# Dummy products in the waits of a gated-mix kernel's start, and a different split of five weight loads over two queues

## The chip, the core and the metric

The kernel runs on one core of a Trainium2 chip. The metric is the device time in microseconds (us) of one execution. Before the change it is 261.29 us, the median of five runs that lie between 261.19 and 261.47 us. One more execution was taken with the hardware profiler, and every row of the profile is from that one.

## The reference

One token block `x` of 2048 rows and 640 columns goes through two branches, which a gate mixes row by row. All arrays are bf16.

```python
g = sigmoid((x * gate_w).sum(-1, keepdims=True))
# branch a: linear attention, 32 heads of 20 columns
q, k, v = split(x @ wqkv)
phi = lambda t: where(t > 0, t + 1, exp(t)) + 1e-6
kv  = einsum("bhsd,bhse->bhde", phi(k), v);  z = phi(k).sum(s)
a   = (phi(q) @ kv / (phi(q) @ z + 1e-6)) @ wo
# branch b: shifted mixer, then an MLP
h  = gelu(layernorm(x) @ w1)
x1 = x + shift_four_column_groups(h) @ w2
b  = x1 + gelu(layernorm(x1) @ w3) @ w4
out = g * a + (1 - g) * b
```

## The kernel before

The 2048 rows are 16 chunks of 128. The order of the work on each engine is the order in which the program is written (`manual_schedule`); engines and queues run beside each other and wait for each other by semaphores.

**The stages.** First comes the projection to `k` for all 16 chunks (`k_mm`, L246, and `k_post`, L251), then `q` in ten units with the products of `phi(k)` and `x` between them, then `w1`, the small products of the attention, `w2`, and at last `w3` and `w4` with the mix. The change touches the loads and the products ahead of the first stage and the first chunk of it.

**The operands of the first stage.** A `k` chunk needs two things. One is the transposed chunk of `x`, in `xT` (the tile RXT): 640 rows on five groups of 128 partitions. The other is the weight for `k`, in `wkg` (the tile RA): five slabs of 128 rows, called wk slab 0 to 4 here, each with 640 columns of weight, one column that holds the gate weight, and one column of ones. So one chunk is 5 x 2 matrix products, one of 512 columns and one of 130 for each slab, added up in one of four PSUM buffers `PP[0]` to `PP[3]`. For chunk c of the loop, ScalarE takes exp and copies the last two columns out, and VectorE finishes `phi` with two instructions.

**How the operands come.** Two queues issue loads, SyncE's (SP) and ScalarE's. ScalarE's queue issues the gate row (`g5`, L160) and then wk slabs 1 and 3. SP's queue issues chunk 0 of `x` as it stands in memory (`load_x`, L155), then wk slabs 0, 2 and 4 (`load_wk`, L164), and then, in `late_loads`, the transposing loads of `x` (`load_xT`, L158): chunks 1 to 5 one by one and chunks 6 to 15 in pairs, which write `xT` directly. Behind these stand the loads of `wq`, the other rows of `x` and the weights of the later stages, all on SP's queue.

**Chunk 0.** It doesn't wait for a transposing load: TensorE transposes it from `x_sb` in five products (L318), VectorE copies three of the results to `xT` (L319) and ScalarE two (L320). The gate row is transposed in the same way (L310) and VectorE puts it into `wkg` (L311). Between these, TensorE multiplies constant ones by ones into a part of PSUM that nothing reads (`warm_up`, L304): three such products of 512 columns at the start, one of 512 and one of 128 behind the gate's transpose, and the same two behind the transposes of `x`. Then the loop over chunks starts at L326.

```python
    load_x(0, 1)
    for (q, dc) in ((aq, 1), (sp, 0), (aq, 3), (sp, 2), (sp, 4)):
        load_wk(q, dc)
```

Of the kernel before, what the change touches and what calls it, by code (L numbers as in the profile page):

```python
# [16 lines left out]
def kernel(  # L17
# [14 lines left out]
    P = 128  # L32
# [3 lines left out]
    NCH = S // P  # L36
    DC = D // P
# [97 lines left out]
    PP = [psum.tile([P, 1024], F32, name=f"pp{i}") for i in range(4)]  # L135
    free = [0, 1, 2, 3]

    def alloc():
        return free.pop(0)

    def release(i):
        free.append(i)

    mm = nc.tensor.matmul
# [6 lines left out]
    sp, aq = nc.sync, nc.scalar  # L151
    xv = x2.rearrange("(c p) d -> p c d", p=P)

    def load_x(c0, c1):
        sp.dma_start(x_sb[:, c0:c1, :], xv[:, c0:c1, :])  # L155
# [7 lines left out]
    def load_wk(q, dc):  # L163
        q.dma_start(wkg[:, dc, 0:D], A_wqkv[dc * P:(dc + 1) * P, D:2 * D])  # L164

    load_x(0, 1)
    for (q, dc) in ((aq, 1), (sp, 0), (aq, 3), (sp, 2), (sp, 4)):
        load_wk(q, dc)


# [66 lines left out]
    def phi(dst, src, n, extra=None):  # L237
        e = eb[ecnt[0] % NE]
        ecnt[0] += 1
        act(e[:, 0:n], src, ACT.Exp)  # L240
        if extra is not None:
            act(extra[0], extra[1], ACT.Copy)
        nc.vector.tensor_scalar(e[:, 0:n], e[:, 0:n], 1.0, 1e-6, op0=ALU.min, op1=ALU.add)  # L243
        nc.vector.scalar_tensor_tensor(dst, src, 0.0, e[:, 0:n], op0=ALU.max, op1=ALU.add)  # L244

    def k_mm(c, p, dc):  # L246
        for (n0, n1) in ((0, 512), (512, KW)):
            mm(PP[p][:, n0:n1], lhsT=xT[:, dc, c * P:(c + 1) * P], rhs=wkg[:, dc, n0:n1],  # L248
               start=(dc == 0), stop=(dc == DC - 1))

    def k_post(c, p):  # L251
        phi(pk[:, c, :], PP[p][:, 0:D], D, (ym[:, c, :], PP[p][:, D:D + 2]))
        release(p)
# [47 lines left out]
    def one(shape):  # L301
        return nc.const_aps.tensor(1.0, shape, BF16)

    def warm_up(n, cols=512):  # L304
        for _ in range(n):
            mm(PP[1][:, 512:512 + cols], lhsT=one([P, P]), rhs=one([P, cols]), start=True, stop=True)

    warm_up(3)
    tg = PP[0][:, 512:1024].bitcast(BF16)
    nc.tensor.transpose(tg[:, 0:DC], g5[0:DC, :], ident[0:DC, 0:DC])  # L310
    nc.vector.tensor_copy(wkg[:, :, D:D + 1], tg[:, 0:DC].rearrange("p (j o) -> p j o", o=1))  # L311
    warm_up(1)
    warm_up(1, 128)

    ta, tb = PP[3][:, 0:512].bitcast(BF16), PP[2][:, 0:512].bitcast(BF16)
    for dc in range(DC):
# [1 line left out]
        nc.tensor.transpose(t[:, k * P:(k + 1) * P], x_sb[:, 0, dc * P:(dc + 1) * P], ident[:])  # L318
    nc.vector.tensor_copy(xT[:, 0:3, 0:P], ta[:, 0:3 * P].rearrange("p (j s) -> p j s", j=3))  # L319
    act(xT[:, 3:5, 0:P], tb[:, 0:2 * P].rearrange("p (j s) -> p j s", j=2), ACT.Copy)  # L320
    warm_up(1)
    warm_up(1, 128)
    free[:] = [1, 0, 3, 2]


    for c in range(NCH):  # L326
        p = alloc()
        for dc in range(DC):
            k_mm(c, p, dc)
        k_post(c, p)  # L330
# [20 lines left out]
    for half in range(2):  # L351
        for j in range(DC):
            p = alloc()
            for dc in range(DC):
                for tt in range(2):
                    t0 = half * 1024 + tt * 512
                    mm(PP[p][:, tt * 512:(tt + 1) * 512], lhsT=wqp[:, dc, j], rhs=xT[:, dc, t0:t0 + 512],  # L357
                       start=(dc == 0), stop=(dc == DC - 1))
# [327 lines left out]
```

## Time and profile before

| what | value |
|---|---|
| median of five runs | 261.29 us (261.19 to 261.47) |
| the profiled execution, device time | 261.53 us |
| the profiled execution, span of the profile | 259.8 us |
| TensorE products, busy | 255.8 us, 98% of the span |
| VectorE busy | 145.3 us, 56% |
| ScalarE busy | 108.4 us, 42% |
| 160 products of the `k` stage (L248), busy | 23.2 us |
| idle time of TensorE just before products of L248 | 0.3 us |

The profile names engines PE (TensorE's products), PEld (TensorE's weight loads), DVE (VectorE), ACT (ScalarE), POOL (GpSimd); SPq and ACTq are the queues of SyncE and ScalarE, whose rows show how long the issue of a load took, not the transfer. A row of the timeline has start and duration in us, engine, line, operation, what it writes and reads, its shape, and how many instructions are merged in it; in brackets stands the idle time before it and what ended that. Products are pipelined, so the duration of one is longer than the distance to the next; rates are read from the starts.

### The profile page before, as it was taken

The page shows a single profiled execution, that of the slowest core. Times are in us where ns is not written, and L with a number is a line of the kernel's source. Part 1 is how long each engine was busy: PE and PEld are TensorE (multiplying, and loading weights), DVE is VectorE, ACT ScalarE, POOL GpSimd, SP SyncE. Part 2 cuts the span into 40 slices and gives each one's busy share as a digit, 9 for nine tenths or more (in the row PEclk, how much of TensorE's full clock was granted, in tenths as well). Part 3 has the DMA queues.
Part 4 walks back from the last instruction along what each step waited for, and adds up shares of the span by engine and source line. Part 5 has one row for each costly group of instructions (what it writes and reads, how often), then busy time and mean ns, then how long its engine had stood idle before and what let it go on. Part 6 is the DMA issues. An engine that isn't in the chain of part 4 may idle for free.

```text
span 259.8 us, 4010 instructions
## 1 busy us (share of the span) xinstructions
PE 255.8 (98%) x1575; PEld 132.4 (51%) x1575; DVE 145.3 (56%) x244; ACT 108.4 (42%) x160; POOL 35.4 (14%) x110
## 2 busy tenths in 40 slices
PE   8999999999999999999999999999999999999995
PEld 3555555454455445554444455555544445555553
DVE  0688758697899999999996025413210002234133
ACT  2555657766356741235886521202034445202200
POOL 3000051243000002547760000000000000000000
DMA  7699997432231269964451000200200000010011
GB/s 199 137 196 298 363 265 171 92 70 53 51 76 28 58 200 377 332 114 48 95 109 29 3 0 0 78 25 0 78 25 0 3 0 0 3 50 25 28 50 50
DMA packets 44364, 24.55 MB, mean 94 GB/s; under 512 B 33122, under 2 KB 43578, under 8 KB 44346
## 3 DMA queue, kind: packets, MB, share of 16 engines
q1 hardware_dynamic: 43904, 23.94, 36.3%
q10 hardware_dynamic: 442, 0.36, 0.4%
q8 instruction: 12, 0.20, 0.3%
q14 instruction: 6, 0.05, 0.1%
HBM read 12.99 MB, written 3.44 MB: 63 GB/s over the span
## 4 chain that ended last, share of the span: by engine, by line
PE 96%; DMA 2%; SPq 1%; DVE 0%; issue 0%
PE pp L598 22%; PE pp L542 20%; PE pp L572 8%; PE pp L527 8%; PE pp L388 8%; PE pp L357 8%; PE pp L248 8%; PE pp L264 7%; PE pp L267 2%; PE pp L551 2%; DMA RXT<-in_A_x_dram 2%; PE pp L604 1%; PE pp L561 1%; PE pp L424 1%; PE pp L411 1%; SPq L164 0%
## 5 line engine op out<-in xcount | busy, mean ns | idle before, releaser
L598 PE MATMUL pp<-RB,RXH 128*128 128x512 bf16 (+1 forms) x416 | 58.6, 299 | 0.0
L542 PE MATMUL pp<-lnxT,RA 128*128 128x512 bf16 x240 | 52.1, 379 | 0.0
L598 PEld LDWEIGHTS <-RXH 128*128 128x128 bf16 x416 | 31.8, 98 | 24.5
L542 PEld LDWEIGHTS <-RA 128*128 128x128 bf16 x240 | 23.4, 98 | 28.1
L544 ACT ACTIVATE RXH<-pp 128x1024 bf16<-128x1024 f32 x24 | 24.1, 1019 | 29.7 <-PE pp L542 29.7
L240 ACT ACTIVATE ebs<-pp 128x640 bf16<-128x640 f32 (+1 forms) x26 | 21.5, 827 | 26.1 <-PE pp L357 14.2
L575 ACT ACTIVATE RXH<-pp,g_all 128x640 f32<-128x640 f32 x16 | 12.7, 795 | 45.4 <-PE pp L572 45.4
L577 DVE SCALAR_TENSOR_TENSOR RPK<-RPK,omg,RXH 128x640 f32<-128x640 f32 x8 | 7.1, 884 | 41.4 <-ACT RXH L575 41.4
L248 PE MATMUL pp<-RA,RXT 128*128 128x512 bf16 (+1 forms) x160 | 23.2, 307 | 0.3 <-DMA RXT<-in_A_x_dram 0.3
L357 PE MATMUL pp<-RXT,RA 128*128 128x512 bf16 x100 | 23.2, 379 | 0.0
L572 PE MATMUL pp<-Mp,pqT 128*128 128x512 bf16 (+1 forms) x160 | 23.1, 299 | 0.0
L527 PE MATMUL pp<-w,RXH 128*128 128x512 bf16 (+1 forms) x160 | 21.9, 299 | 0.0
L577 DVE SCALAR_TENSOR_TENSOR RXT<-RXT,omg,RXH 128x640 f32<-128x640 f32 x8 | 7.1, 885 | 21.4 <-ACT RXH L575 21.4
L264 PE MATMUL pp<-RPK,RXH 128*128 128x512 bf16 x80 | 18.6, 379 | 0.0
L248 PEld LDWEIGHTS <-RXT 128*128 128x128 bf16 x160 | 12.7, 100 | 10.8 <-issue 1.1
L388 PE MATMUL pp<-lnxT,RB 128*128 128x512 bf16 x80 | 17.9, 379 | 0.0
L243 DVE TENSOR_SCALAR ebs<-ebs 128x640 bf16<-128x640 bf16 (+1 forms) x26 | 9.6, 368 | 14.5 <-ACT ebs L240 13.4
L572 PEld LDWEIGHTS <-pqT 128*128 128x128 bf16 x160 | 12.3, 98 | 9.8 <-issue 0.4
L527 PEld LDWEIGHTS <-RXH 128*128 128x128 bf16 x160 | 12.3, 98 | 9.6
L357 PEld LDWEIGHTS <-RA 128*128 128x128 bf16 x100 | 11.5, 117 | 9.8
L244 DVE SCALAR_TENSOR_TENSOR RPK<-pp,ebs 128x640 bf16<-128x640 f32 x16 | 13.2, 825 | 2.1
L582 DVE SCALAR_TENSOR_TENSOR RXH<-pp,omg,RXT 128x640 bf16<-128x640 f32 x8 | 6.9, 882 | 13.3 <-PE pp L598 8.3
(102 smaller groups left out, 255.4 us busy)
## 6 DMA issues: line engine op xcount, KB each, us to landing
out_dram<-RXH SPq DMA_DIRECT2D x15, 160.0 KB, 1.8
RA<-in_B_w_dram SPq DMA_DIRECT2D x5, 432.0 KB, 6.1
RA<-in_A_wqkv_dram SPq DMA_DIRECT2D x2, 800.0 KB, 9.4
RXH<-in_A_x_dram SPq DMA_DIRECT2D x3, 480.0 KB, 8.5
RB<-in_B_w_dram SPq DMA_DIRECT2D x1, 1120.0 KB, 10.1
RXH<-in_A_x_dram SPq DMA_DIRECT2D x3, 320.0 KB, 7.9
RB<-in_B_w_dram SPq DMA_DIRECT2D x1, 960.0 KB, 11.7
RB<-in_B_w_dram SPq DMA_DIRECT2D x1, 800.0 KB
```

Of the source, the lines that this page charges most:

```text
L240: act(e[:, 0:n], src, ACT.Exp)
L244: nc.vector.scalar_tensor_tensor(dst, src, 0.0, e[:, 0:n], op0=ALU.max, op1=ALU.add)
L248: mm(PP[p][:, n0:n1], lhsT=xT[:, dc, c * P:(c + 1) * P], rhs=wkg[:, dc, n0:n1], start=(dc == 0), stop=(dc == DC - 1))
L264: mm(PP[p][:, 0:512], lhsT=x_sb[:, c, i * P:(i + 1) * P], rhs=pk[:, c, 0:512], **st)
L357: mm(PP[p][:, tt * 512:(tt + 1) * 512], lhsT=wqp[:, dc, j], rhs=xT[:, dc, t0:t0 + 512], start=(dc == 0), stop=(dc == DC - 1))
L388: mm(PP[p][:, tt * 512:(tt + 1) * 512], lhsT=lh, rhs=lnxT[:, dc, t0:t0 + 512], start=(dc == 0), stop=(dc == DC - 1))
L527: mm(PP[p][:, n0:n1], lhsT=hsT[:, fc, 2 + c * P:2 + (c + 1) * P], rhs=w2[:, fc, n0:n1], start=(fc == 0), stop=(fc == DC - 1))
L542: mm(PP[p][:, k * 512:(k + 1) * 512], lhsT=w3[:, dc, (fc + k) * P:(fc + k + 1) * P], rhs=lnxT[:, dc, t * 512:(t + 1) * 512], start=(dc == ...
L544: act(h2T[:, t % 2, fc:fc + 2, :], PP[p][:].rearrange("p (k s) -> p k s", k=2), ACT.Gelu_apprx_tanh)
L572: mm(PP[p][:, n0:n1], lhsT=pqT[:, j, c * P:(c + 1) * P], rhs=Mp[:, j, n0:n1], start=(j == 0), stop=(j == DC - 1))
L577: nc.vector.scalar_tensor_tensor(x1(c), x1(c), omg[:, c:c + 1], ga, op0=ALU.mult, op1=ALU.add)
L598: mm(PP[ps[m]][:, n0:n1], lhsT=h2T[:, k, fc, i * P:(i + 1) * P], rhs=w4[:, fc, n0:n1], start=(m < 2 and fc == 0), stop=(m >= 2 and fc == N ...
```

## The change

It has two parts.

The loads: ScalarE's queue issues the gate row and wk slab 1. SP's queue issues chunk 0 of `x` and then wk slabs 0, 2, 3 and 4, and the transposing loads behind them.

The dummy products: `warm_up` becomes `fill`, which takes a list of widths and a PSUM buffer. There are four products of 512 columns at the start where there were three, one of 512 behind the gate's transpose where there were one of 512 and one of 128, and, as before, one of 512 and one of 128 behind the transposes of `x`. Chunk 0 is taken out of the loop, and two dummy products of 128 columns are put behind its slabs 0, 1 and 4, into `PP[0]`, which chunk 1 uses next. Chunk 0 still uses `PP[1]`, and the other chunks use the same buffers as before.

```diff
     load_x(0, 1)
-    for (q, dc) in ((aq, 1), (sp, 0), (aq, 3), (sp, 2), (sp, 4)):
+    for (q, dc) in ((aq, 1), (sp, 0), (sp, 2), (sp, 3), (sp, 4)):
         load_wk(q, dc)
...
-    def warm_up(n, cols=512):
-        for _ in range(n):
-            mm(PP[1][:, 512:512 + cols], lhsT=one([P, P]), rhs=one([P, cols]), start=True, stop=True)
-
-    warm_up(3)
+    def fill(*cols, p=1):
+        for n in cols:
+            mm(PP[p][:, 0:n], lhsT=one([P, P]), rhs=one([P, n]), start=True, stop=True)
+
+    fill(512, 512, 512, 512)
...
-    warm_up(1)
-    warm_up(1, 128)
+    fill(512)
...
-    warm_up(1)
-    warm_up(1, 128)
-    free[:] = [1, 0, 3, 2]
+    fill(512, 128)
+    free[:] = [0, 3, 2]
+    for dc in range(DC):
+        k_mm(0, 1, dc)
+        if dc < 2 or dc == 4:
+            fill(128, 128, p=0)
+    k_post(0, 1)
...
-    for c in range(NCH):
+    for c in range(1, NCH):
         p = alloc()
```

## The prediction

> **What bounds the kernel now.** I read the page's first part, then the chain that ended last cut to the first 24 us, then the timelines of TensorE and of both queues for the first 14 us, and last how long single transposing loads took to land.
>
> ```profile
> PE 255.8 (98%) x1575; PEld 132.4 (51%) x1575; DVE 145.3 (56%) x244; ACT 108.4 (42%) x160; POOL 35.4 (14%) x110
> ```
>
> TensorE is the bound of the whole: 255.8 of 259.8 us. The idle time is at both ends, so a change at the start is worth exactly what it does to the moment from which TensorE never waits again. The chain says when that is and what sets it.
>
> ```profile
> 1.72 0.42 SPq L164
> 2.14 0.04 issue
> 2.18 0.44 SPq L164
> 2.62 0.04 issue
> 2.67 4.28 DMA RXT<-in_A_x_dram
> 6.95 0.05 issue
> 6.99 17.05 PE pp L248 x123
> ```
>
> Columns: start, duration, what. From 6.99 us on TensorE runs; ahead of it stands no product and no wk slab as such, but the first transposing load (chunk 1), issued at 2.67 us, right behind SP's third slab, and landed at 6.95. Chunk 0 is off this chain, as the timeline of TensorE shows:
>
> ```profile
> 0.83 1.44 PE L306 MATMUL pp<-const-bfloat16-1.0 128*128 128x512 bf16 x3 [0.83 <-PEq L670]
> 2.20 0.18 PE L310 MATMUL pp<-ident,g 5*128 5x5 bf16 x1
> 2.32 0.71 PE L306 MATMUL pp<-const-bfloat16-1.0 128*128 128x512 bf16 x2
> 3.17 0.72 PE L318 MATMUL pp<-ident,RXH 128*128 128x128 bf16 x5
> 3.67 0.74 PE L306 MATMUL pp<-const-bfloat16-1.0 128*128 128x512 bf16 x2
> 4.21 2.52 PE L248 MATMUL pp<-RA,RXT 128*128 128x512 bf16 x10
> 6.99 7.24 PE L248 MATMUL pp<-RA,RXT 128*128 128x512 bf16 x51 [0.27 <-DMA RXT<-in_A_x_dram]
> ```
>
> The ten products of chunk 0 start at 4.21 and are done at 6.73; then TensorE waits 0.27 us for chunk 1's `xT`. So chunk 0 can become 0.27 us longer before anyone feels it, and making it shorter brings nothing. The transposing loads feed the chunks behind it:
>
> ```profile
> 2.67 11.55 SPq L158 DMA_TRANSPOSE RXT<-in_A_x_dram  x8
> ```
>
> SP's queue is busy with them without a hole; single ones start at 2.67, 4.03, 5.33, 6.65, 7.97 and 9.30 (the pair 6 and 7), 1.26 to 1.39 us each. A chunk takes TensorE 1.36 us (ScalarE's exps of successive chunks start at 8.57, 9.93, 11.29 and 12.65). Issue and use go at nearly the same pace, so loads keep the small lead they begin with. The pair 6 and 7 is the tightest:
>
> ```profile
> L158 SPq DMA_TRANSPOSE RXT<-in_A_x_dram x1: 1390/1390/1390, 9.3 to 9.3; - x1
> DMA to landing us min/median/max: 4.5/4.5/4.5
> ```
>
> 9.30 + 4.5 = 13.80 us. TensorE is through chunk 5 at 6.99 + 5 x 1.36 = 13.79, and the weight-load row shows that it did wait there:
>
> ```profile
> 13.84 1.20 PEld L248 LDWEIGHTS <-RXT 128*128 128x128 bf16 x10 [0.20 <-DMA RXT<-in_A_x_dram]
> ```
>
> The others have slack (uses at 6.99 plus 1.36 for each chunk before): chunk 4 lands at 6.65 + 3.6 = 10.25 for a use at 11.07, the pair 8 and 9 at 10.73 + 4.4 = 15.1 for 16.5, the pair 10 and 11 at 12.17 + 5.8 = 18.0 for 19.2. So there are two gates, `xT` of chunk 1 at 6.95 and of the pair 6 and 7 at 13.80, and both hang on SP's queue. After 20 us no row of waits shows TensorE's products waiting for data.
>
> **The change part by part.**
>
> *SP's queue.* It issues one more wk slab ahead of the first transposing load. Slabs there start at 1.25, 1.72, 2.18 and the next issue at 2.67, so one slab costs 0.46 to 0.49 us; I take 0.47. Every transposing load, and everything behind on the queue, is issued 0.47 us later: chunk 1 at 3.14, the pair 6 and 7 at 9.77. Nothing else of the queue changes. What is issued later than the transposes (`wq` at 17.99) lands some us ahead of its use, and I cost it at nothing; were that cover gone, it would cost the same 0.47, not on top of it.
>
> *Does a later issue mean a later landing?* Here the trace gives two different answers for the two gates. This row is the busy share of the DMA engines in slices of 0.5 us from 0 to 20:
>
> ```profile
> DMA  0004977999999393391872799689999799299996
> ```
>
> From 3.5 to 6.5 us they are full, moving slabs and then chunk 1. Chunk 1 landed 4.28 us after its issue where chunk 3 took 2.9, so it was queued behind the slabs. The bytes ahead of it are the same five slabs after the change. Bounds for its landing: 6.95 if the engines alone set it, 7.42 if the issue does; I take 7.1, nearer the first, because of the full slices. At 6.5, 7.5 to 8.5, 9.0 and 10.5 us the slices are nearly empty (1 to 3 tenths): the backlog is gone, and the loads of chunks 4, 5 and the pair 6 and 7 go at the pace of the issue. For the pair I take the whole shift: landing at 14.27, TensorE at 14.31 instead of 13.84. That is +0.47 us there, whatever chunk 1 did earlier, as long as chunk 1 starts less than 0.47 later; the two delays are not added. Its bounds: the pair's 4.5 us is the long end of these rows (2.9, 3.6, 4.3, 4.4), so with 3.6 it would land at 13.4 and cost nothing.
>
> *ScalarE's queue.* One issue less, 0.44 us. What stands behind it is a table load (2.26, 1.28 us) and then the copy L320, which waits for the transposes of `x` until 3.92. It gains nothing.
>
> *Dummy products up to 4.21.* A fourth product of 512 columns costs 0.43 us (the three of 0.83 to 2.2 stand 0.38 and 0.43 apart). They end near 2.49, so the gate's transpose goes from 2.20 to about 2.49, and the 512 behind it runs until 3.03. The transposes of `x` wait for its load until 3.16 anyway, so nothing moves: cost 0, cover 0.13 us. VectorE's copy of the gate column goes from 2.42 to about 2.75, and it is needed at 4.6.
>
> *Dummy products in chunk 0.* Six of 128 columns. The transposes of 128 columns start 0.107 us apart at this stage (3.25, 3.36, 3.46, 3.57). At that price four of them, behind slabs 0 and 1, cost 0.43 us, and the last two 0.21. But single starts in chunk 0 show the rate doubling: two 512-column products follow at 0.43 us (4.21 to 4.63, 4.75 to 5.17), the last ones like this:
>
> ```profile
> 5.84 0.56 PE L248 MATMUL pp<-RA,RXT 128*128 128x512 bf16 x1
> 6.23 0.44 PE L248 MATMUL pp<-RA,RXT 128*128 128x130 bf16 x2
> 6.29 0.44 PE L248 MATMUL pp<-RA,RXT 128*128 128x512 bf16 x2
> 6.51 0.22 PE L248 MATMUL pp<-RA,RXT 128*128 128x130 bf16 x1
> ```
>
> 512 columns take 0.22 us from 6.29 to 6.51, 130 columns 0.06: full rate from about 6.2 us, although the profile's own clock column says 1.00 throughout. With the full rate again from 6.2, chunk 0 runs: slab 0 to 4.75, fill to 4.96, slab 1 to 5.50, fill to 5.71, slab 2 to 6.23, slab 3 to 6.50, slab 4 to 6.77, fill to 6.88. Slabs land, before, at 2.18 + 3.7 = 5.9 at the latest, so they are in time even 0.4 later. At 6.88 chunk 0 is still ahead of chunk 1's `xT`: cost 0. If the full rate came only at 7.0, it would end near 7.27; if never, 4.21 + 5 x 0.54 + 6 x 0.107 = 7.55, which is 0.56 past 6.99. Nothing can be gained by a faster chunk 0, since `xT` is not there.
>
> The Trainium skill, TensorE: Matmul & The Clock Gate, "What's actually happening", says that the rate doubles after a busy window of about 3.4 us that runs free of the kernel's start, so that another execution may double sooner or later than 6.2. By it the fills could only bring the doubling forward, worth at most an estimated 0.1 us here; no row of this single trace shows the phase. A rule that speaks against the change is in DMA: Bandwidth & Descriptors, "Issuing engines are not separate DMA queues": several issuing engines save only the time of the issue itself, usually small beside the transfer. Here that time is the 0.47 us given up, and it isn't small beside a lead of nothing.
>
> *Sum.* Against the profiled execution: +0.47 at the pair 6 and 7, 0 for the rest: 261.53 + 0.47 = 262.00. The profiled execution is 0.24 above the median, so on the median it is 261.29 + 0.47 = 261.76 us.
>
> **The rivals.**
>
> *B, hidden (the change does nothing to the end).* Chunk 1 lands near 6.95 since the engines are full, and the pair lands in 3.6 to 4.0 us rather than 4.5. For it: the spread of landings. Against it: both pairs behind it took over 4.4. Chunk 0's end at 6.88 to 7.2 is then what counts: 0 to +0.2, 261.3 to 261.5 us.
>
> *C, slower by more than the issue.* Place: chunk 1's `xT`. With four slabs on one queue and one on the other, the two queues no longer fill the engines together; slab 4 and the transposes behind it come later than the issue alone says, or a late full rate stretches chunk 0 to 7.55. It decides from a start of chunk 1 at 7.52 on (6.99 + 0.53). For it: the slices of 2.5 to 3.5 us, with SP's slab alone, are only 7 tenths full. Against: chunk 1 has a shorter queue when issued later. Price: +0.55 to +0.9, 261.85 to 262.2 us.
>
> *D, faster.* The pair 6 and 7 and chunk 1 both land 0.5 us sooner though issued later, and a full rate ahead of 5 us lets chunk 0 end by 6.4: 260.5 to 261.1 us. Against it: three things would have to go right at once.
>
> **How the numbers follow.** A (the 0.47) 0.45, B 0.29, C 0.20, D 0.06. About 0.2% (0.52 us) is what a measurement of this kernel can tell from no change. A lies just inside; runs scatter by 0.1 us or so around it, so some 0.05 of A falls outside, and D's slow end is within: faster 0.05, same 0.70, slower 0.25. The range leaves out half of D and half of C: 261.1 to 262.05.
>
> **What would show it.** SP's rows: four slabs from 1.25 and the first L158 near 3.14. TensorE's start of chunk 1 between 7.0 and 7.45, and a wait for RXT near 14.3, with the chain's dense piece beginning there or at chunk 1. TensorE's gaps ahead of 4.2 us filled without the transposes of `x` moving from 3.17. I am wrong if the first L158 is not later, if the pair's landing doesn't follow its issue, or if a slab, not `xT`, is what TensorE waits for.

## The result, and the profile after

The changed kernel takes 262.07 us in the median of 44 runs (261.73 to 263.3); the kernel before, run beside it, 261.52 us in the median of 79 (261.19 to 263.19). The ratio is 1.0018, with a 95% interval of 1.0011 to 1.0024: some 0.3 to 0.6 us slower. The profiled executions say the same: 261.96 against 261.53 us, spans 260.2 and 259.8.

TensorE is as busy as before, 0.1 us apart. The page's first part:

```profile
PE 255.9 (98%) x1581; PEld 132.9 (51%) x1581; DVE 145.2 (56%) x244; ACT 108.5 (42%) x160; POOL 34.9 (13%) x110
```

The chain that ended last, cut to the first 24 us (start, duration, what):

```profile
2.18 0.44 SPq L164
2.62 0.04 issue
2.67 0.43 SPq L164
3.10 0.04 issue
3.14 4.25 DMA RXT<-in_A_x_dram
7.39 0.05 issue
7.44 16.74 PE pp L248 x121
```

It has one more slab on SP's queue (2.67, 0.43 us), the first transposing load is issued at 3.14 instead of 2.67, and the dense run of TensorE begins at 7.44 instead of 6.99. The load itself took 4.25 us where it took 4.28, so between these two profiles the shift of the issue came through whole.

The timeline of TensorE up to chunk 1:

```profile
0.83 1.86 PE L306 MATMUL pp<-const-bfloat16-1.0 128*128 128x512 bf16 x4 [0.83 <-PEq L673]
2.62 0.18 PE L310 MATMUL pp<-ident,g 5*128 5x5 bf16 x1
2.74 0.61 PE L306 MATMUL pp<-const-bfloat16-1.0 128*128 128x512 bf16 x1
3.14 0.74 PE L317 MATMUL pp<-ident,RXH 128*128 128x128 bf16 x5
3.67 0.74 PE L306 MATMUL pp<-const-bfloat16-1.0 128*128 128x512 bf16 x2
4.72 0.69 PE L248 MATMUL pp<-RA,RXT 128*128 128x512 bf16 x2 [0.31 <-DMA RA<-in_A_wqkv_dram]
...
6.73 0.28 PE L306 MATMUL pp<-const-bfloat16-1.0 128*128 128x128 bf16 x2
7.44 7.75 PE L248 MATMUL pp<-RA,RXT 128*128 128x512 bf16 x55 [0.43 <-DMA RXT<-in_A_x_dram]
```

The dummy products fill the gaps ahead of 4.2 us, and the transposes of `x` stand where they stood. Chunk 0 waits 0.31 us for slab 0 and with all its dummy products is still done at 7.0, 0.43 us before its successor's data. The last gate, the pair 6 and 7, by its rows of RXT:

```profile
L158 SPq DMA_TRANSPOSE RXT<-in_A_x_dram x1: 1387/1387/1387, 9.8 to 9.8; - x1
DMA to landing us min/median/max: 4.3/4.3/4.3
```

Issued at 9.77, landed at 14.07. TensorE, which started chunk 1 at 7.44, needs it at 7.44 + 6.81 = 14.25 (five chunks of 1.3625 us; ScalarE's exps start at 9.01, 10.37, 11.74, 13.10 and 14.46). So in this execution it didn't wait there: between 6 and 20 us the list of waits has a single one of weight loads for RXT, 0.6 us, at chunk 1.

### The profile page after: what moved, and what is told of

Same layout as the page of the kernel before. It is cut to its first block, busy times and chain, and to the rows that moved or that the text cites. A ratio compares the mean times of both kernels' runs of the same rounds, so it can differ in the third digit from the quotient of the medians.

```text
span 260.2 us, 4022 instructions
## 1 busy us (share of the span) xinstructions
PE 255.9 (98%) x1581; PEld 132.9 (51%) x1581; DVE 145.2 (56%) x244; ACT 108.5 (42%) x160; POOL 34.9 (13%) x110
## 4 chain that ended last, share of the span: by engine, by line
PE 96%; DMA 2%; SPq 1%; issue 0%; DVE 0%
PE pp L601 22%; PE pp L545 20%; PE pp L575 8%; PE pp L530 8%; PE pp L391 8%; PE pp L360 8%; PE pp L248 8%; PE pp L264 7%; PE pp L267 2%; PE pp L554 2%; DMA RXT<-in_A_x_dram 2%; PE pp L607 1%; PE pp L564 1%; SPq L164 1%; PE pp L427 1%; PE pp L414 1%
```

## The experiments

Every kernel is the one before with the edit shown, unless something else is said. "Before" in a ratio means runs of the kernel before on the same chip. A ratio is an estimate from all the runs of both kernels, with its 95% interval behind it; it can differ from the quotient of the two medians by 0.001 to 0.002. Each kernel was profiled once, unless a second profile is named. Where only the list of slabs in the loop over `load_wk` differs, the list alone is given in place of a diff.

### One part of the change at a time

The new loads with the old dummy products:

```diff
-    for (q, dc) in ((aq, 1), (sp, 0), (aq, 3), (sp, 2), (sp, 4)):
+    for (q, dc) in ((aq, 1), (sp, 0), (sp, 2), (sp, 3), (sp, 4)):
```

> The new split of the loads with the old dummy products. Theory A (the issue on SP's queue sets the end): the first transposing load is issued at 3.14 us instead of 2.67, chunk 1 starts 0.4 to 0.5 us later than the 6.99 of before, and the time is 0.4 to 0.5 us above that of before, as in the changed kernel. Theory B (the dummy products inside chunk 0 set the end, the load of chunk 1 only happens to land there): no difference to before, within 0.1 us.

Measured: 262.10 us against 261.53, ratio 1.0016 (1.0005 to 1.0028). Its chain:

```profile
3.14 4.30 DMA RXT<-in_A_x_dram
7.44 0.05 issue
7.49 16.52 PE pp L248 x120
```

The new dummy products with the old loads (all of the change's diff but the list of slabs):

> The new dummy products with the old split of the loads. Theory A: no difference to before within 0.15 us; the ten products and six dummy products of chunk 0 end at 6.9 us or earlier, chunk 1 still starts at about 7.0. Theory B: 0.4 to 0.5 us above before, with TensorE busy with chunk 0 until about 7.4.

Measured: 261.55 us against 261.53, ratio 0.9992 (0.998 to 1.0004). Its timeline of TensorE at the end of chunk 0:

```profile
6.74 0.28 PE L306 MATMUL pp<-const-bfloat16-1.0 128*128 128x128 bf16 x2
6.91 8.29 PE L248 MATMUL pp<-RA,RXT 128*128 128x512 bf16 x59
```

Chunk 0 with its six dummy products ends just when chunk 1's data is there (landed at 6.86); the row of chunk 1 has no wait. In this execution slab 0 came 0.26 us late, and the chain that ended last goes through it, chunk 0 and the dummy products, no longer through chunk 1's load:

```profile
1.25 3.39 DMA RA<-in_A_wqkv_dram
...
6.90 0.11 PE pp L306 x2
7.02 17.18 PE pp L248 x125
```

So the cover of the dummy products was just used up here. Theory B falls all the same: the loads alone make the change's loss, and the dummy products cost nothing that the runs show.

### More and fewer slabs on SP's queue

All five on SP's queue: `((sp, 0), (sp, 1), (sp, 2), (sp, 3), (sp, 4))`.

> Old dummy products, all five slabs on SP's queue, in order 0 to 4; ScalarE's queue has the gate row alone. Theory A: first transposing load issued near 3.6, chunk 1 starts near 7.9, 0.8 to 1.0 us above before. Theory C (the DMA engines' traffic ahead of chunk 1 sets its landing, not the issue): the same slabs are ahead of it whatever queue they are on, so it lands at 6.9 to 7.2 and the time is within 0.2 us of before.

Measured: 262.39 us, ratio 1.0029 (1.0018 to 1.004), 0.5 to 1.0 us above before. In its chain the load of chunk 1 takes less time than before:

```profile
3.60 4.04 DMA RXT<-in_A_x_dram
7.64 0.05 issue
7.69 16.33 PE pp L248 x117
```

Two on SP's queue: `((aq, 1), (sp, 0), (aq, 3), (sp, 2), (aq, 4))`.

> Old dummy products, SP's queue has slabs 0 and 2 only, ScalarE's queue 1, 3 and 4. Theory A: first transposing load issued near 2.2, it lands near 6.5, and the end of chunk 0 at about 6.73 is the next gate: 0.2 to 0.3 us below before. The pair 6 and 7, issued 0.47 earlier too, doesn't bind. Theory C: chunk 1 lands at 6.8 to 7.0 as before, since the slabs fill the engines until 5.3 us: within 0.15 us of before.

Measured: 261.43 us, ratio 0.9996 (0.9981 to 1.0011), not to be told from before, though the profiled execution has 261.24 us and a span of 259.5. Its chain:

```profile
2.18 4.51 DMA RXT<-in_A_x_dram
6.69 0.05 issue
6.74 17.29 PE pp L248 x125
```

With two, three, four and five slabs the first transposing load is issued at 2.18, 2.67, 3.14 and 3.60 and lands at 6.69, 6.95, 7.44 and 7.64. In these four profiles three slabs are worth 1.42 us of issue and 0.95 of landing. That two thirds of the shift arrive is not shown by it: with the loads of before unchanged, this load took 3.9 to 4.3 us in four profiles, and with two slabs on SP's queue 4.5, 4.5 and 5.5 in three (the kernels follow below), differences of about the size of the missing third or more. What decides between the theories is the times: against the 261.53 of before, one slab more on SP's queue gave 262.10 and two gave 262.39, where theory C had all within 0.2 us. So theory C falls, and for the sizes theory A holds (0.57 and 0.86 us), though with five slabs chunk 1 started at 7.69 and not near 7.9.

### The traffic ahead of chunk 1's load

The loads of the change, old dummy products, slabs 2 to 4 cut to a tenth of their columns:

```diff
+    for dc in (2, 3, 4):
+        nc.vector.memset(wkg[:, dc, 64:D], 0.0)
     def load_wk(q, dc):
-        q.dma_start(wkg[:, dc, 0:D], A_wqkv[dc * P:(dc + 1) * P, D:2 * D])
+        n = D if dc < 2 else 64
+        q.dma_start(wkg[:, dc, 0:n], A_wqkv[dc * P:(dc + 1) * P, D:D + n])
```

> The new split of the loads with the old dummy products, but slabs 2, 3 and 4 bring 64 of their 640 columns (the rest is set to zero), so the output is not the reference's: five issues on the queues as in the changed kernel, with 432 KB less traffic ahead of chunk 1's transposing load. If the issue sets that load's landing, it still lands at 7.2 to 7.5 and the time is 0.4 us above before. If the traffic does, it lands 2.9 to 3.6 us after its issue at 3.14, at 6.0 to 6.7; chunk 1 then starts at 6.5 to 6.8, and the pair 6 and 7, issued at 9.77, becomes the gate at 13.8 to 14.3: 0 to 0.4 above before.

Measured: 261.83 us against 261.72, ratio 1.0008 (0.9999 to 1.0017). The load of chunk 1, issued at 3.13, lands 3.7 us later (4.3 with full slabs) and chunk 1 starts at 6.84, between the two expectations. By this one profile the traffic of the slabs is worth 0.6 us of its landing, not far beyond the 0.4 us by which this load differs between profiles with the loads of before. The chain doesn't go through chunk 1 any more:

```profile
9.76 4.29 DMA RXT<-in_A_x_dram
14.05 0.05 issue
14.09 9.93 PE pp L252 x71
```

The pair 6 and 7, issued 0.46 us later than before, is what TensorE waits for. With chunk 1 out of the way the second gate still holds a part of the loss: the profiled execution is at 261.77 us, 0.24 above that of before, where the changed kernel's is 0.43 above. In the medians it is 0.11 us, and the interval reaches 1.

### The two gates apart

One small load of a later stage between the transposing loads of chunks 1 and 2:

```diff
-        for c in range(1, 6):
-            load_xT(c, c + 1)
+        load_xT(1, 2)
+        for g in range(1):
+            sp.dma_start(w2[32 * g:32 * (g + 1), 4, :], B_w2[CG * g + P:CG * (g + 1), :])
+        for c in range(2, 6):
+            load_xT(c, c + 1)
...
-        for g in range(4):
+        for g in range(1, 4):
```

> The kernel before with one small load of a later stage (32 rows of w2, 40 KB) issued between the transposing load of chunk 1 and that of chunk 2, about 0.46 us of SP's queue. It parts the two gates: chunk 1 is untouched, chunks 2 to 15 are issued 0.46 later. Theory A2 (the pair 6 and 7 alone carries the shift to the end): chunk 1 starts at 7.0, TensorE waits 0.2 to 0.45 us ahead of chunk 6, time +0.2 to +0.45. Theory A1 (chunk 1 alone carries it): within 0.15 us of before.

Measured: 261.97 us against 261.72, ratio 1.0012 (1.0 to 1.0023). The size is what theory A2 said, but not the place. The experiment didn't part the gates: chunk 1's own load, issued at 2.66 as before, took 4.77 us.

```profile
2.66 4.77 DMA RXT<-in_A_x_dram
7.42 0.05 issue
7.47 16.74 PE pp L248 x121
```

In the same run chunk 0 waited 0.63 us for a slab, too. Whether the 40 KB behind it did that, or this execution's loads were slow anyhow, one profile can't tell; loads as slow (slabs of 4.8 and 4.9 us, chunk 1's load of 5.5) stand also in a profile further down of a kernel without the small load. The runs say more. None of the 11 is below 261.75 us, where 17 of the 33 of before are. The pair 6 and 7, issued at 9.84, landed at 14.03 in this profile; by the account below that allows no start before 7.25, a span of 260.05 us, and some 261.75 of device time (which is 1.7 us more than the span in these profiles). A floor of just this height is what A2 asks for. It doesn't rule out that the small load held up chunk 1's load in each run.

What shows the pair as a gate by itself is a second look at the new dummy products with the old loads, made for another reason (the scatter of its runs):

> The kernel with the new dummy products and the old split of the loads once more, for its scatter. If the dummies narrow it: again no run above 262.0, and a median 0 to 0.2 us below that of before. If the first twelve runs were luck: two or three runs above 262.0 as in before, and the same median.

Measured: 261.48 us against 261.62, ratio 0.9996 (0.9979 to 1.0014); three of the twelve runs are above 262.0. So that none was above in the first twelve was luck, and no narrowing by the dummy products is shown. In its profile the load of chunk 1 landed early, 3.9 us after its issue at 2.66, and chunk 1 started at 6.56. TensorE then gave all of it back:

```profile
6.56 6.99 PE L248 MATMUL pp<-RA,RXT 128*128 128x512 bf16 x49
13.80 1.48 PE L248 MATMUL pp<-RA,RXT 128*128 128x512 bf16 x9 [0.26 <-DMA RXT<-in_A_x_dram]
```

The pair 6 and 7 came at 13.75 as it did before (13.80), and the span is 259.8 as before.

All of it in one account. The dense run counts from the later of two moments, the start of chunk 1, and the start that the pair 6 and 7 allows (its landing plus 0.04, less five chunks, 6.81):

| kernel | chunk 1 starts | pair allows | later one | span | difference |
|---|---|---|---|---|---|
| before | 6.99 | 7.03 | 7.03 | 259.8 | 252.8 |
| changed | 7.44 | 7.30 | 7.44 | 260.2 | 252.8 |
| new loads alone | 7.49 | 7.45 | 7.49 | 260.3 | 252.8 |
| new dummies alone | 6.91 | 6.8 | 6.91 | 259.7 | 252.8 |
| the same, again | 6.56 | 6.98 | 6.98 | 259.8 | 252.8 |
| two slabs on SP's queue | 6.74 | 6.53 | 6.74 | 259.5 | 252.8 |
| light slabs | 6.84 | 7.28 | 7.28 | 260.1 | 252.8 |
| small load in between | 7.47 | 7.25 | 7.47 | 260.2 | 252.7 |

The last column is constant to about the tenth that the span is given in: nothing behind these two gates differs between the kernels. It doesn't tell why a load landed when it did. The kernel with five slabs on SP's queue fits as well, if a third gate is counted: it started chunk 1 at 7.69 and waited another 0.13 us ahead of chunk 5 (260.6 - 7.82 = 252.8). So do the kernels below in which the end of chunk 0 or a slab was the gate: chunk 1 started at 7.71, 6.85 and 7.98 in spans of 260.5, 259.6 and 260.7.

### Two other bounds

SP's queue with one slab, ScalarE's with four: `((aq, 1), (sp, 0), (aq, 2), (aq, 3), (aq, 4))`.

> Old dummy products, SP's queue has slab 0 alone, ScalarE's queue 1, 2, 3 and 4. First transposing load issued near 1.7 us. If each slab on SP's queue is worth what it was from two to four slabs, it lands near 6.4. The table load on ScalarE moves 0.9 later, and with it the copy of two of chunk 0's transposes, to about 4.4. The gate is then the end of chunk 0 near 6.5 to 6.75: time equal to that with two slabs on SP's queue, 0.2 to 0.35 below before.

Measured: 262.58 us against 261.72, ratio 1.0045 (1.0022 to 1.0068), a clear miss: 1.2 us slower by the ratio (0.9 by the medians) where 0.2 to 0.35 faster was expected. Its chain goes through a slab:

```profile
2.27 0.45 ACTq L164
2.72 0.04 issue
2.76 4.90 DMA RA<-in_A_wqkv_dram
7.66 0.04 issue
7.71 16.45 PE pp L248 x119
```

Slab 4, issued at 2.76 on ScalarE's queue, took 4.9 us to land, where slabs took 3.1 to 3.7 before. The transposing loads on SP's queue start at 1.72 in this kernel and run beside the slabs. That they held the slabs up is not shown: slabs took 4.4 to 4.5 us with the small load in between, and 4.8 and 4.9 in one of three profiles with two slabs on SP's queue. Chunk 0, which had 0.27 us to spare, became the gate: TensorE stood 1.07 us ahead of slab 3 (7.16) and started slab 4 at 7.71.

No dummy products at all (`for _ in range(0)` in `warm_up`):

> The kernel before without any dummy product. TensorE idles ahead of 4.2 us, so the full rate comes later than the 6.2 of before, by up to some 3 us. Chunk 0 at half rate throughout ends near 6.95, and each us at half rate after chunk 1's start costs half a us: 0 to 1.2 us above before. If the dummy products did nothing, no difference to before and products 0.22 us apart from the same moment on.

Measured: 262.75 us against 261.72, ratio 1.002 (0.9994 to 1.0046), with runs from 261.54 to 263.78. The profiled execution (261.96 us) is 0.43 above before's. Its chain has no wait for `xT` at all:

```profile
1.24 3.06 DMA RA<-in_A_wqkv_dram
4.30 0.04 issue
4.35 19.85 PE pp L248 x131
```

From 4.35 on TensorE runs without a stop, at half rate at first: a 512-column product that starts at 7.51 still takes 0.43 us until the next one starts, where 0.22 was the distance from 6.3 on before. Seven of the 12 runs are above 262.5 us, and five of the 33 of before. So dummy products look worth having, but the interval of the ratio doesn't settle it; for the new ones, beyond those of before, no gain in the median shows at all.

### A version that is faster than both

Two slabs on SP's queue as above, together with the new dummy products:

> The new dummy products with slabs 0 and 2 on SP's queue and 1, 3 and 4 on ScalarE's. If chunk 1's transposing load is what the dense run waits for, it is there by 6.7 and the end of chunk 0 with its dummies, near 6.9, is the gate: 0 to 0.15 us below before in a run like the profiled one. If the new dummy products also make TensorE reach its full rate at about the same moment in each run, the runs scatter less than those of before: their upper quarter ends below 261.7, where that of before is at 261.8, and no run in twelve is above 262.0, where about a fifth of before's are.

Measured: 261.36 us against 261.62, ratio 0.9983 (0.9966 to 1.0001); two of twelve runs above 262.0. One of these two is the profiled one, in which the load of chunk 1 took 5.5 us and a slab was late by 1.38 us as well.

The same without the dummy products inside chunk 0:

```diff
     for dc in range(DC):
         k_mm(0, 1, dc)
-        if dc < 2 or dc == 4:
-            fill(128, 128, p=0)
     k_post(0, 1)
```

> The same loads, with the new dummy products ahead of chunk 0 and none inside it. Chunk 0 ends near 6.6, chunk 1's load lands near 6.7: 0.2 to 0.3 us below before in a run like the profiled one. If the dummies ahead of chunk 0 are enough for an even full rate, no run in twelve is above 262.0; if those inside chunk 0 are what does it, two or three are.

Measured: 261.31 us against 261.62, ratio 0.9973 (0.9954 to 0.9992), no run of twelve above 262.0. From chunk 0 on its timeline of TensorE has no wait left (some records of products are missing from this trace, none of the starts shown):

```profile
4.21 10.97 PE L248 MATMUL pp<-RA,RXT 128*128 128x512 bf16 x69
```

It is the only one of the eleven comparisons whose interval lies below 1, and by little. Its edit to the loads goes the other way from the change: one slab fewer on SP's queue instead of one more. That the dummies ahead of chunk 0 narrow the scatter is not shown by twelve runs, after the first twelve of another kernel misled.

## Why the prediction was right

- **The sum.** 0.47 us was forecast, and the ratio of 1.0018 is 0.47 us of 261.5; with an interval of 0.29 to 0.63 us, the agreement to the hundredth is luck. No change beyond 0.2% was its likeliest outcome, and 1.0018 is just inside. The absolute 261.76 stood on a median of five runs, which lies 0.23 below that of the 79; on theirs the same sum gives 261.52 + 0.47 = 261.99, and 262.07 was measured, 0.02 above the range given with the lower base.
- **SP's queue.** One slab costs 0.47 us, and the transposing loads up to the pair 8 and 9 are later by it: 3.14 and 9.77, as worked out. The pairs behind came 0.56 to 0.93 us later, which nothing waited for.
- **Which gate: wrong in the profile.** The step "*Does a later issue mean a later landing?*" put chunk 1 at 7.1, as held up by full DMA engines rather than by its issue, and let the pair 6 and 7 at 14.27 carry the loss. In the profiled execution it was chunk 1 that bound, landing at 7.39 (7.44 with the new loads alone), and the pair, 4.3 us after its issue and not 4.5, came at 14.07 with 0.18 us to spare. With chunk 1 at 7.1 as forecast, this pair would have allowed a start at 7.30 where 7.03 was allowed before, a loss of 0.27 us and not 0.47: that the profile showed nearly the whole shift is owed to the gate that the forecast had let off. Which of the two bound in the other 43 runs is not known; in the profiles they are 0.14 and 0.04 us apart with the new loads. The full slices were real, but with the new loads the landing came as late as the issue in both profiles. The sum survived because both gates hang on the same queue, 0.04 us apart before.
- **The pair as a second gate: right.** It bound in the light-slab kernel (14.05) and in the second look at the new dummies (13.75), and ended any gain at chunk 1 there. Its load took 4.2 to 4.5 us in all profiles, a much smaller spread than chunk 1's.
- **ScalarE's queue and the dummy products at nothing: right.** The dummies alone give 0.9992 and 0.9996 with intervals around 1. The cover of 0.27 us was read from the modelled end of chunk 0's last product, 6.73; by the starts, it was through at 6.57 and the cover was 0.43. The forecast end of chunk 0 was 6.88; by the starts (the last dummy product and 0.06 us) it was 6.85 in the first profile of the dummies alone and in the changed kernel, with slab 0 late by 0.26 and 0.31 us, and 6.47 in the second profile. The gate's transpose came at 2.62 where 2.49 was forecast, which moved nothing.
- **The clock.** The full rate came at about 6.2 us before, at 5.7 in the changed kernel, and near 5.4 in the second profile of the new dummies with the old loads where the first had it near 5.7. With two slabs on SP's queue and the same dummies ahead of chunk 0 it was there with chunk 0's first product at 4.2 us in one profile (512 columns took 0.22 us), and came near 6.7 in the other, without dummies inside chunk 0. So no run shows that the new dummies fix the moment. The Trainium skill, TensorE: Matmul & The Clock Gate, "What's actually happening", has the window that decides this run free of the kernel's start, and these different moments in one and the same kernel agree with it. It changed nothing in the changed kernel's profile, because chunk 0 was not the gate; where it was, in the kernel without dummies inside chunk 0, the half rate put chunk 1's start at 6.85 though its load had landed at 6.66.
- **The queues.** The Trainium skill, DMA: Bandwidth & Descriptors, "Issuing engines are not separate DMA queues", says that loads of all queues run on the same DMA engines and interleave, so that spreading them saves issue time alone. The issue time was the price of the change, as the prediction weighed it. That loads of two queues hold each other up no run here shows for itself: the slab of 4.9 us beside the transposing loads, with four slabs on ScalarE's queue, is within what slabs took elsewhere (up to 4.9).
- **Rivals.** B's spread of landings exists (3.7 to 5.6 us for chunk 1's load in these profiles) but didn't hide the shift in the median. C's mechanism, slabs that come late, is not what bound in the changed kernel; it is what bound with four slabs on ScalarE's queue.

## What to carry to other kernels

When an engine is dense from some moment to the end, read what sets that moment and what would set it next, as an "effective start" for each gate; the span then follows to a tenth of a us, and work put into a wait ahead of it changes nothing. A queue that issues back to back with hardly any lead over its reader passes an extra issue on to the end (here 0.57 us for one slab more and 0.86 for two, by the medians), and all gates on that queue are issued later together. Moving issues to another queue can help until the moved loads themselves become the gate: here one slab moved off SP's queue was neutral (and gave a small gain together with dummies ahead of chunk 0), two moved off cost 1.2 us. And one profile is one execution: a load's landing moved by up to a us between profiles of the same loads, so what a shift of its issue is worth is read from the runs.

## What the runs showed that was not expected

- A slab issued at 2.76 us on ScalarE's queue took 4.9 us to land while transposing loads ran on SP's; the slabs of the kernel before took 3.1 to 3.7. With two slabs on SP's queue, the same five loads had slabs of at most 3.8 and 4.0 us in two profiles and of 4.9 in a third.
- The transposing load of chunk 1 took between 3.7 and 5.6 us in thirteen profiles, of kernels in which nothing but the loads and dummy products around it differ, and 3.9 and 4.2 in two profiles of one and the same kernel. That of the pair 6 and 7 took 4.2 to 4.5.
- Without dummy products the runs of one kernel lay between 261.54 and 263.78 us; with those of before, most were within 0.5 us of each other.
